# Routed attention and an ELU layer on one core: scores and value products in blocks of six, over one ring of PSUM banks

## The chip, the core and the metric

The kernel runs on one core of one Trainium2 chip. A core has a matrix engine (TensorE; its products are listed as PE and its weight loads as PEld), VectorE (DVE), ScalarE (ACT), GpSimd (POOL) and SyncE (SP, which issues DMAs here). Each engine works through its own queue in order, and engines wait for one another by semaphores. TensorE writes only to PSUM, which has eight banks of 128 partitions by 512 fp32 values in this kernel; GpSimd is given no PSUM operand anywhere in it. The metric is the device time of one execution in microseconds (us).

## The reference

Queries, keys and values have the shape batch 4, heads 8, sequence 768, head dimension 64. Every query and key is assigned to the nearest of 16 centroids of its head, and a query sees only the keys of its own cluster. The result, as 3072 tokens of 512 numbers, goes through a two-layer network with an ELU between.

```python
q_assign = argmax(einsum('bhsd,hcd->bhsc', q_n, c_n))   # q, k and centroids normalised
k_assign = argmax(einsum('bhsd,hcd->bhsc', k_n, c_n))
mask   = q_assign[:, :, :, None] == k_assign[:, :, None, :]
scores = where(mask, q @ k.T / 8, -1e9)
attn   = softmax(scores)                                  # over the keys
x      = (attn @ v) as (3072, 512)
h      = x @ w_in                                         # (3072, 2048)
g      = where(h > 0, h, exp(min(h, 0)) - 1)
out    = g @ w_out                                        # (3072, 512)
```

All arrays are fp32 in the kernel; w_in and w_out arrive as 8-byte numbers and are converted on the chip.

## The kernel before, in words

Everything that matters here is in `main_path`. The heads are taken in pairs (NPR = 4 pairs a batch, 16 in all). A pair's 768 queries are taken in two halves of HS = 384 columns, its keys in NT = 6 tiles of 128. One **score unit** is one key tile of one half of one pair, for both heads: `score` (L305) issues, for the two heads e = 0 and 1, an fp32 product of 64 rows (L311) and a bf16 product that adds the mask (L320: the key's cluster against the query's, a large negative number where they differ), each a head in its own half of the array's rows. Both heads' results lie in two neighbouring PSUM banks, and one exponential on ACT (L328) turns them into a tile `p` of 128 x 768 in SBUF. An fp32 product is issued as two instructions, so a unit has four of L311 and two of L320. `add` (L330) sums the six `p` of a half, on POOL for batch 1 and on DVE later. `values` (L340) multiplies the unit's `p` with the values, the two heads in the two halves of the array's columns (four instructions of L345), into one bank `o` over the six tiles; after the sixth ACT copies it to `xT` (L354). `divide` (L356) sums over the keys with a product with ones (L360), ACT moves the sums and keeps a check sum (L365), DVE takes the reciprocal (L366), POOL multiplies `xT` by it (L368) and keeps another sum (L369).

`mlp` (L372) is the two-layer network for one half of one batch: 16 steps `hidden` (L377; eight instructions of L383 into one bank, then exponential on ACT L392, clamp on POOL L393, and on DVE L398, which is issued one step later and still reads the bank), then three output tiles `outer` (L403), each in four parts of eight instructions (L413), a copy on ACT (L422) and a DMA out.

`prepare` (L280) plans what the next batch needs: turns of q and k by TensorE against an identity (L231, 3 transposes each) with copies on ACT (L234) and DVE (L236), similarities with the centroids (L247, L254), and the assignment on DVE (L261 to L272); `masks` (L274) makes the queries' mask operand of a pair (L278).

The order is written out by hand: `tc.manual_schedule()` keeps the order in which the program issues. The loop at L462 goes over batches b = 0 to 4, and each has 48 slots. A slot issues one score unit of batch b, then what was set for this slot with `at`: the add of one slot ago, the values of two slots ago (LAG = 2), the divide of a half that ended three slots ago; then, in the first two rounds, two steps of the weights' conversion (`weigh`, DVE and POOL, L185 to L198), then the planned steps for batch b + 1, then 1 or 2 of the 56 steps (`hidden` or `outer` part) of batch b - 1. So TensorE alternates between three tilings of its array in every slot: 64 rows x 128 columns (scores), 128 x 64 (values, divide), 128 x 128 (network, turns). The last round, b = 4, has no scores: it only finishes the network of the last batch.

PSUM is four pools: `ps_s` with 2 tiles of 2 banks for scores, `ps_b` with 2 tiles of 1 bank for `bank()` (turns, similarities, divide, hidden), `ps_o` with 1 for values and `ps_f` with 1 for the outputs; in the last round `hidden` and `outer` also take from `ps_s` and `ps_o` in turn. `p` has 6 buffers, `xT` 10, `gT` 16.

Of the kernel before, what the change touches and what calls it, by code (L numbers as in the profile page):

```python
# [9 lines left out]
F32 = mybir.dt.float32  # L10
# [50 lines left out]
def main_path(ctx, tc, c, q, k, v, centroids, moe_w_in, moe_w_out, out):  # L61
    nc = tc.nc
    B, H, S, D = q.shape
    NC = centroids.shape[1]
    DM, DF = moe_w_in.shape
    NT = S // P
    HT = NT // 2
    HS = S // 2
    NPR = H // 2
    KC = DM // P  # L70
    FC = DF // P
    SCALE = 1.0 / 8.0
# [18 lines left out]


    pairs = [(b, pr) for b in range(B) for pr in range(NPR)]
# [129 lines left out]
    T, sim, hot, qm = {}, {}, {}, {}  # L223
# [76 lines left out]
        return plan  # L300


    pu, osum, den, o_ps, xT = {}, {}, {}, {}, {}

    def score(i, half, kt):  # L305
        b, pr = pairs[i]
        s = ps_s.tile([P, 2, 512], F32, name="scores", tag="s")
        cols = slice(half * HS, (half + 1) * HS)
        for e in range(2):
            rows = slice(64 * e, 64 * e + 64)  # L310
            nc.tensor.matmul(  # L311
                s[:, e, :HS],
                lhsT=T[i, 1][rows, ts(kt, P)],
                rhs=T[i, 0][rows, cols],
                start=True,
                stop=False,
            )
        for e in range(2):
            rows = slice(64 * e, 64 * e + 64)
            nc.tensor.matmul(  # L320
                s[:, e, :HS],
                lhsT=hot[b, 1][rows, ts(kt, P)],
                rhs=qm[i][rows, cols],
                start=False,
                stop=True,
            )
        p = pu[i, half, kt] = probs.tile([P, 2, HS], F32, name="p", tag="p")
        nc.scalar.activation(p, s[:, :, :HS], Act.Exp, scale=SCALE)  # L328

    def add(i, half, kt, eng):  # L330
        if kt == 0:
            return
        if kt == 1:
            osum[i, half] = work.tile([P, 2, HS], F32, name="psum", tag="psum")
        to = osum[i, half]
        eng.tensor_tensor(  # L336
            to, pu[i, half, 0] if kt == 1 else to, pu[i, half, kt], op=Alu.add
        )

    def values(i, half, kt):  # L340
        if kt == 0:
            o_ps[i, half] = ps_o.tile([P, 512], F32, name="o", tag="o")
        o = o_ps[i, half]
        for e in range(2):
            nc.tensor.matmul(  # L345
                o[64 * e : 64 * e + 64, :HS],
                lhsT=raw["v", i][:, e, kt],
                rhs=pu[i, half, kt][:, e],
                start=(kt == 0),
                stop=(kt == NT - 1),  # L350
            )
        if kt == NT - 1:
            x = xT[i, half] = xtp.tile([P, HS], F32, name="xT", tag="xT")
            nc.scalar.copy(x, o[:, :HS])  # L354

    def divide(i, half):  # L356
        s = osum.pop((i, half))
        d = bank()
        for e in range(2):
            nc.tensor.matmul(  # L360
                d[64 * e : 64 * e + 64, :HS], lhsT=ones, rhs=s[:, e], start=True, stop=True
            )
        r = work.tile([P, HS], F32, name="r", tag="r", bufs=1)
        n = 2 * i + half
        nc.scalar.activation(r, d[:, :HS], Act.Copy, accum_out=d_sum[:, n : n + 1])  # L365
        nc.vector.reciprocal(r, r)  # L366
        x = xT[i, half]
        nc.gpsimd.tensor_tensor(x, x, r, op=Alu.mult)  # L368
        nc.gpsimd.tensor_tensor(r_sum, r_sum, r, op=Alu.add)  # L369


    def mlp(b, half, last):  # L372

        g = {}
        lag = []

        def hidden(f):  # L377
            if last and f % 2:
                h = ps_s.tile([P, 2, 512], F32, name="h2", tag="s")[:, 0, :HS]
            else:  # L380
                h = bank()[:, :HS]
            for ch in range(KC):
                nc.tensor.matmul(  # L383
                    h,
                    lhsT=w_in[:, ch, ts(f, P)],
                    rhs=xT[b * NPR + ch, half],
                    start=(ch == 0),
                    stop=(ch == KC - 1),
                )
# [12 lines left out]

        def outer(t, part, o):  # L403
            for step in lag:
                step()
            lag.clear()
            if part == 0:
                if last and t % 2:
                    o[t] = ps_o.tile([P, DM], F32, name="o2", tag="o")
                else:  # L410
                    o[t] = ps_f.tile([P, DM], F32, name="f", tag="f")
            for f in range(4 * part, 4 * part + 4):
                nc.tensor.matmul(  # L413
                    o[t],
                    lhsT=g[f][:, ts(t, P)],
                    rhs=w_out[:, f],
                    start=(f == 0),
                    stop=(f == FC - 1),
                )
            if part == 3:  # L420
                o_sb = work.tile([P, DM], F32, name="o_sb", tag="o_sb")
                nc.scalar.copy(o_sb, o[t])  # L422
# [5 lines left out]
        o = {}  # L428
# [12 lines left out]
    def weigh(n):  # L441
        for _ in range(n):
            step = next(rest, None)
            if step:
                step()
# [5 lines left out]
            step()  # L451
        weigh(1)

    LAG = 2
    slots = 2 * NPR * NT
    later = {}
    now = 0

    def at(n, step):
        later.setdefault(n, []).append(step)  # L460

    for b in range(B + 1):  # L462
        steps = []
        if b > 0:
            for half in range(2):
                steps.extend(mlp(b - 1, half, b == B))
        plan = prepare(b + 1) if b + 1 < B else {}
        done = 0
        for n in range(slots):
            if b < B:  # L470
                i, half, kt = b * NPR + n // (2 * NT), (n // NT) % 2, n % NT
                if n % (2 * NT) == LAG + 2 and i + 1 < len(pairs):
                    load("v", i + 1)
                if n % (2 * NT) == 2 * NT - 4 and pairs[i][1] + 1 < NPR:
                    masks(i + 1)
                score(i, half, kt)
                eng = nc.gpsimd if b == 0 else nc.vector
                at(now + 1, lambda i=i, half=half, kt=kt, eng=eng: add(i, half, kt, eng))
                at(now + LAG, lambda i=i, half=half, kt=kt: values(i, half, kt))
                if kt == NT - 1:  # L480
                    at(now + LAG + 1, lambda i=i, half=half: divide(i, half))
            for step in later.pop(now, []):
                step()
            if b == 0:
                weigh(2)
            for step in plan.get(n, []):
                step()
            upto = (n + 1) * len(steps) // slots
            for step in steps[done:upto]:
                step()  # L490
            done = upto
            now += 1
            if b == 1:
                weigh(2)
    weigh(1000)


# [238 lines left out]
```

## Time and profile before

| what | us |
|---|---|
| median of 3 runs | 1281.11 (1281.02 to 1281.29) |
| the profiled execution, its own time | 1280.53 |
| its span, first to last instruction | 1278.8 |
| busy: PE products | 1132.8 (89%) |
| busy: DVE | 494.5 (39%) |
| busy: POOL | 296.7 (23%) |
| busy: ACT | 281.8 (22%) |

The profile is of one execution. A line of a group names the source line, engine, operation, what it writes and reads by the program's names, the shape and the count, and then its busy time and the mean of one in ns. A line of the chain of waits has a start, a length and the work that held up the end in that time; x8 says that eight instructions stand in that piece. Matmuls overlap in the trace: a product's own duration is longer than the distance to the next one, so lengths in the chain, which go from start to start, are the ones to add up. "before" in brackets behind a line of the timeline is the idle time ahead of it and what ended it. Line numbers are those of the kernel before.

### The profile page before, as it was taken

To read this page: it belongs to the slowest core of one execution; us is meant where nothing else is said; L and a number is where in the kernel's file an instruction comes from. 1 tells how busy PE (TensorE), PEld (TensorE's weight loads), DVE (VectorE), ACT (ScalarE), POOL (GpSimd) and SP (SyncE) were. 2 spreads that over 40 slices of the span, in tenths; PEclk is the share of its full clock that TensorE was granted. 3 is DMA by queue.
4 is the path that set the end of the run, shared out by engine and by line. 5 is a ranking of instruction groups with operands and counts; after the bars stand their busy time and mean duration, and the time that the engine had idled before them with its cause. 6 is when DMAs were issued, how large, how long until landed. Compare 5 with 4: busy or idle time off the path is not lost.

```text
span 1278.8 us, 10641 instructions
## 1 busy us (share of the span) xinstructions
PE 1132.8 (89%) x4291; PEld 486.1 (38%) x4291; DVE 494.5 (39%) x596; ACT 281.8 (22%) x475; POOL 296.7 (23%) x303
## 2 busy tenths in 40 slices
PE   4644444799999999999999999999999999999998
PEld 2211111244433443344434443344434443454553
DVE  5888888833321335223321335223322332220110
ACT  2221212232212221223212321222212321110110
POOL 2476666552110220012110210012111210110110
PEclk9877777899999999999999999999999999999999
DMA  9423233010101010010100000000000000000000
GB/s 225 122 83 104 73 111 91 30 37 1 37 17 46 1 37 9 9 46 1 37 17 21 1 13 9 8 21 1 13 17 21 1 1 15 11 1 17 9 1 27
DMA packets 62793, 42.75 MB, mean 33 GB/s; under 512 B 51472, under 2 KB 55568, under 8 KB 62736
## 3 DMA queue, kind: packets, MB, share of 16 engines
q1 hardware_dynamic: 62736, 41.98, 11.5%
q8 instruction: 36, 0.59, 0.2%
q14 instruction: 21, 0.17, 0.0%
HBM read 35.68 MB, written 6.29 MB: 33 GB/s over the span
## 4 chain that ended last, share of the span: by engine, by line
PE 78%; POOL 8%; DVE 7%; issue 4%; ACT 2%; SPq 1%; DMA 0%; ACTq 0%; POOLq 0%
PE f L413 25%; PE bank L383 24%; PE scores L311 10%; PE o L345 8%; POOL psum L336 4%; PE h L383 3%; PE o L413 2%; PE scores L320 2%; DVE r L366 1%; PE bank L360 1%; PE bank L247 1%; DVE ex L187 1%; PE bank L231 1%; DVE kT L236 1%; POOL w_out L198 1%
## 5 line engine op out<-in xcount | busy, mean ns | idle before, releaser
L413 PE MATMUL f<-w_out,gT 128*128 128x512 f32 x704 | 320.4, 602 | 4.1 <-ACT o_sb L422 4.1
L383 PE MATMUL bank<-xT,w_in 128*128 128x384 f32 x896 | 314.2, 496 | 8.3 <-DVE kT L236 5.2
L328 ACT ACTIVATE p<-scores 128x768 f32<-128x768 f32 x192 | 155.8, 812 | 370.5 <-PE scores L320 363.1
L383 PEld LDWEIGHTS bank<-xT,w_in 128*128 128x128 f32 x896 | 163.1, 190 | 150.9 <-DVE gT L398 23.9
L413 PEld LDWEIGHTS f<-w_out,gT 128*128 128x128 f32 x704 | 128.3, 190 | 181.5 <-issue 171.9
L393 POOL TENSOR_SCALAR gT<-gT 128x384 f32<-128x384 f32 x128 | 64.8, 506 | 528.4 <-ACT gT L392 528.4
L311 PE MATMUL scores<-qT,kT 64*128 64x384 f32 x768 | 179.6, 545 | 0.0
L345 PE MATMUL o<-p,v_raw 128*64 128x384 f32 x768 | 170.0, 522 | 0.0
L366 DVE RECIPROCAL r<-r 128x384 f32<-128x384 f32 x32 | 81.7, 2552 | 216.5 <-ACT r L365 216.5
L398 DVE SCALAR_TENSOR_TENSOR gT<-gT,bank 128x384 f32<-128x384 f32 x112 | 61.7, 551 | 260.6 <-POOL gT L393 260.6
L336 DVE TENSOR_TENSOR psum<-psum,p 128x768 f32<-128x768 f32 x96 | 105.3, 1097 | 91.8 <-ACT p L328 91.4
L392 ACT ACTIVATE gT<-bank 128x384 f32<-128x384 f32 x112 | 55.0, 491 | 301.1 <-PE bank L383 301.1
L368 POOL TENSOR_TENSOR xT<-xT,r 128x384 f32<-128x384 f32 x32 | 46.3, 1448 | 316.0 <-DVE r L366 316.0
L360 PE MATMUL bank<-psum,ones 128*64 128x384 f32 x128 | 31.8, 579 | 91.1 <-DVE kT L236 48.9
L311 PEld LDWEIGHTS scores<-qT,kT 64*128 64x128 f32 x768 | 59.1, 188 | 121.4 <-issue 119.3
L345 PEld LDWEIGHTS o<-p,v_raw 128*64 128x64 f32 x768 | 42.2, 138 | 92.5 <-issue 92.5
L320 PE MATMUL scores<-qm,hot 64*128 64x384 bf16 x384 | 64.0, 326 | 8.2 <-DVE qm L278 8.2
L336 POOL TENSOR_TENSOR psum<-psum,p 128x768 f32<-128x768 f32 x32 | 58.8, 1837 | 1.0
L187 DVE TENSOR_SCALAR ex<-words 128x512 uint32<-128x512 uint32 x32 | 50.2, 1567 | 21.9 <-POOL w_out L198 11.5
L236 DVE COPY kT<-bank 128x384 f32<-128x384 f32 x32 | 17.1, 554 | 83.8 <-PE bank L231 83.8
L360 PEld LDWEIGHTS bank<-psum,ones 128*64 128x64 f32 x128 | 7.0, 147 | 106.8 <-issue 62.5
L369 POOL TENSOR_TENSOR r_sum<-r_sum,r 128x384 f32<-128x384 f32 x32 | 47.5, 1485 | 0.0
(78 smaller groups left out, 575.0 us busy)
## 6 DMA issues: line engine op xcount, KB each, us to landing
words<-in_moe_w_in_dram SPq DMA_DIRECT2D x16, 512.0 KB, 3.9
words<-in_moe_w_out_dram SPq DMA_DIRECT2D x16, 512.0 KB, 3.5
q_raw<-in_q_dram SPq DMA_DIRECT2D x32, 192.0 KB, 3.7
k_raw<-in_k_dram SPq DMA_DIRECT2D x32, 192.0 KB, 4.0
v_raw<-in_v_dram SPq DMA_DIRECT2D x16, 384.0 KB, 4.1
out_dram<-o_sb SPq DMA_DIRECT2D x24, 256.0 KB, 2.0
cen<-in_centroids_dram SPq DMA_DIRECT2D x1, 32.0 KB, 1.8
```

Of the source, the lines that this page charges most:

```text
L187: nc.vector.tensor_scalar(ex, high, 20, 0x7FF, op0=Alu.logical_shift_right, op1=Alu.bitwise_and)
L311: nc.tensor.matmul(s[:, e, :HS], lhsT=T[i, 1][rows, ts(kt, P)], rhs=T[i, 0][rows, cols], start=True, stop=False,)
L320: nc.tensor.matmul(s[:, e, :HS], lhsT=hot[b, 1][rows, ts(kt, P)], rhs=qm[i][rows, cols], start=False, stop=True,)
L328: nc.scalar.activation(p, s[:, :, :HS], Act.Exp, scale=SCALE)
L336: eng.tensor_tensor(to, pu[i, half, 0] if kt == 1 else to, pu[i, half, kt], op=Alu.add)
L345: nc.tensor.matmul(o[64 * e : 64 * e + 64, :HS], lhsT=raw["v", i][:, e, kt], rhs=pu[i, half, kt][:, e], start=(kt == 0), stop=(kt == NT - 1),)
L366: nc.vector.reciprocal(r, r)
L383: nc.tensor.matmul(h, lhsT=w_in[:, ch, ts(f, P)], rhs=xT[b * NPR + ch, half], start=(ch == 0), stop=(ch == KC - 1),)
L392: nc.scalar.activation(t, h, Act.Exp)
L393: nc.gpsimd.tensor_scalar(t, t, 1.0, 0.0, op0=Alu.min, op1=Alu.max)
L398: lambda: nc.vector.scalar_tensor_tensor(t, t, -1.0, h, op0=Alu.add, op1=Alu.max)
L413: nc.tensor.matmul(o[t], lhsT=g[f][:, ts(t, P)], rhs=w_out[:, f], start=(f == 0), stop=(f == FC - 1),)
```

## The change

PSUM becomes one tile `ring` of six banks and the two single banks `o_bank` and `f_bank`; `bank()` hands out the ring's banks in turn, and `banks()` two neighbours, starting at an even one. `score` takes a range of key tiles. `values` calls `divide` itself, right after its last tile. `mlp` yields eight groups a batch: per half two of eight hidden steps, each with its own `finish`, then two of six output parts, in an order in which t = 1 alone uses `f_bank` and t = 0 and t = 2 share `o_bank` with the values.

In the loop, a block of G = 6 units replaces the slot for b = 1 to 4: first the values of the last block and its divide (`flush(0)`), then six score units, the masks of the next pair, the adds, and then the eight hidden steps or six output parts of one group, with the planned steps for the next batch spread between these. For b = 0, G is 1: a slot issues its score unit, the add of the same unit, the values that are two units late (and at the sixth the divide with them), two weight steps, and the planned steps. In both, values are loaded at the slot or block that holds position 3 of a pair instead of at position 4, and masks come after the scores, at position 9 instead of 8.

```diff
-    ps_s = ctx.enter_context(tc.tile_pool(name="ps_s", bufs=2, space=PSUM))
-    ps_b = ctx.enter_context(tc.tile_pool(name="ps_b", bufs=2, space=PSUM))
-    ps_o = ctx.enter_context(tc.tile_pool(name="ps_o", bufs=1, space=PSUM))
-    ps_f = ctx.enter_context(tc.tile_pool(name="ps_f", bufs=1, space=PSUM))
+    psum = ctx.enter_context(tc.tile_pool(name="psum", bufs=1, space=PSUM))
...
+    NB = 6
+    ring = psum.tile([P, NB, 512], F32, name="ring")
+    o_bank = psum.tile([P, 512], F32, name="o_bank")
+    f_bank = psum.tile([P, 512], F32, name="f_bank")
+    turn_of = [0]
+
+    def banks():
+        turn_of[0] += turn_of[0] % 2
+        n = turn_of[0] % NB
+        turn_of[0] += 2
+        return ring[:, n : n + 2]
+
     def bank():
-        return ps_b.tile([P, 512], F32, name="bank", tag="b")
+        n = turn_of[0] % NB
+        turn_of[0] += 1
+        return ring[:, n]
...
-    def score(i, half, kt):
+    def score(i, half, kts):
...
-        s = ps_s.tile([P, 2, 512], F32, name="scores", tag="s")
+        for kt in kts:
+            s = banks()
...
     def values(i, half, kt):
-        if kt == 0:
-            o_ps[i, half] = ps_o.tile([P, 512], F32, name="o", tag="o")
-        o = o_ps[i, half]
...
-            nc.scalar.copy(x, o[:, :HS])
+            nc.scalar.copy(x, o_bank[:, :HS])
+            divide(i, half)
...
         def hidden(f):
-            if last and f % 2:
-                h = ps_s.tile([P, 2, 512], F32, name="h2", tag="s")[:, 0, :HS]
-            else:
-                h = bank()[:, :HS]
+            h = bank()[:, :HS]
...
-        def outer(t, part, o):
-            for step in lag:
-                step()
-            lag.clear()
...
+        def outer(t, part):
+            o = f_bank if t == 1 else o_bank
...
-        for f in range(FC):
-            yield lambda f=f: hidden(f)
-        for t in range(HT):
-            for part in range(4):
-                yield lambda t=t, part=part: outer(t, part, o)
+        for n in range(0, FC, FC // 2):
+            yield [lambda f=f: hidden(f) for f in range(n, n + FC // 2)] + [finish]
+        for parts in (
+            [(0, 0), (0, 1), (0, 2), (0, 3), (1, 0), (1, 1)],
+            [(2, 0), (2, 1), (2, 2), (2, 3), (1, 2), (1, 3)],
+        ):
+            yield [lambda t=t, part=part: outer(t, part) for t, part in parts]
...
+    units = 2 * NPR * NT
+    pending = []
+
+    def flush(left):
+        while len(pending) > left:
+            values(*pending.pop(0))
...
+        G = NT if b else 1
+        for n in range(0, units, G):
+            if b:
+                flush(0)
             if b < B:
                 i, half, kt = b * NPR + n // (2 * NT), (n // NT) % 2, n % NT
+                kts = range(kt, kt + G)
+                within = range(n % (2 * NT), n % (2 * NT) + G)
+                if 3 in within and i + 1 < len(pairs):
                     load("v", i + 1)
+                score(i, half, kts)
+                pending.extend((i, half, x) for x in kts)
+                if 2 * NT - 3 in within and pairs[i][1] + 1 < NPR:
                     masks(i + 1)
+                for x in kts:
+                    add(i, half, x, nc.vector if b else nc.gpsimd)
+            if b == 0:
+                flush(2)
+                weigh(2)
+            beside = [step for m in range(n, n + G) for step in plan.get(m, [])]
+            main = groups[n // G] if b else []
+            done = 0
+            for m, step in enumerate(main):
                 step()
+                upto = len(beside) * (m + 1) // len(main)
+                for other in beside[done:upto]:
+                    other()
+                done = upto
+            for other in beside[done:]:
+                other()
```

More of the change, by code (lines that the diff above doesn't have):

```diff
@@ L300, in prepare @@
         return plan
-    pu, osum, den, o_ps, xT = {}, {}, {}, {}, {}
-    def score(i, half, kt):
+    pu, osum, xT = {}, {}, {}
+    def score(i, half, kts):
         b, pr = pairs[i]
-        s = ps_s.tile([P, 2, 512], F32, name="scores", tag="s")
         cols = slice(half * HS, (half + 1) * HS)
[L309 to L328, printed above, removed]
+        for kt in kts:
+            s = banks()
+            for e in range(2):
+                rows = slice(64 * e, 64 * e + 64)
+                nc.tensor.matmul(
+                    s[:, e, :HS],
+                    lhsT=T[i, 1][rows, ts(kt, P)],
+                    rhs=T[i, 0][rows, cols],
+                    start=True,
+                    stop=False,
+                )
+            for e in range(2):
+                rows = slice(64 * e, 64 * e + 64)
+                nc.tensor.matmul(
+                    s[:, e, :HS],
+                    lhsT=hot[b, 1][rows, ts(kt, P)],
+                    rhs=qm[i][rows, cols],
+                    start=False,
+                    stop=True,
+                )
+            p = pu[i, half, kt] = probs.tile([P, 2, HS], F32, name="p", tag="p")
+            nc.scalar.activation(p, s[:, :, :HS], Act.Exp, scale=SCALE)
     def add(i, half, kt, eng):
@@ L340, in values @@
     def values(i, half, kt):
-        if kt == 0:
-            o_ps[i, half] = ps_o.tile([P, 512], F32, name="o", tag="o")
-        o = o_ps[i, half]
         for e in range(2):
             nc.tensor.matmul(
-                o[64 * e : 64 * e + 64, :HS],
+                o_bank[64 * e : 64 * e + 64, :HS],
                 lhsT=raw["v", i][:, e, kt],
@@ L372, in mlp @@
     def mlp(b, half, last):
-        g = {}
-        lag = []
+        g, lag = {}, []
         def hidden(f):
-            if last and f % 2:
-                h = ps_s.tile([P, 2, 512], F32, name="h2", tag="s")[:, 0, :HS]
-            else:
-                h = bank()[:, :HS]
+            h = bank()[:, :HS]
             for ch in range(KC):
@@ L393, in hidden @@
             nc.gpsimd.tensor_scalar(t, t, 1.0, 0.0, op0=Alu.min, op1=Alu.max)
-            for step in lag:
-                step()
-            lag.clear()
+            finish()
             lag.append(
@@ L401, in hidden, with finish @@
             )
-        def outer(t, part, o):
+        def finish():
             for step in lag:
@@ L406, in outer @@
             lag.clear()
[L407 to L411, printed above, removed]
+        def outer(t, part):
+            o = f_bank if t == 1 else o_bank
             for f in range(4 * part, 4 * part + 4):
                 nc.tensor.matmul(
-                    o[t],
+                    o,
                     lhsT=g[f][:, ts(t, P)],
@@ L421, in outer @@
                 o_sb = work.tile([P, DM], F32, name="o_sb", tag="o_sb")
-                nc.scalar.copy(o_sb, o[t])
+                nc.scalar.copy(o_sb, o)
                 nc.sync.dma_start(
@@ L426, in outer @@
                 )
-        o = {}
-        for f in range(FC):
-            yield lambda f=f: hidden(f)
-        for t in range(HT):
-            for part in range(4):
-                yield lambda t=t, part=part: outer(t, part, o)
+        for n in range(0, FC, FC // 2):
[5 more added lines that the diff above has]
+            yield [lambda t=t, part=part: outer(t, part) for t, part in parts]
     load("v", 0)
@@ L452, in main_path @@
         weigh(1)
[L454 to L460, printed above, removed]
+    units = 2 * NPR * NT
[3 more added lines that the diff above has]
+            values(*pending.pop(0))
     for b in range(B + 1):
-        steps = []
+        groups = []
         if b > 0:
             for half in range(2):
-                steps.extend(mlp(b - 1, half, b == B))
+                groups.extend(mlp(b - 1, half, b == B))
@@ L467, in main_path @@
         plan = prepare(b + 1) if b + 1 < B else {}
-        done = 0
-        for n in range(slots):
+        G = NT if b else 1
+        assert b == 0 or len(groups) == units // G
+        for n in range(0, units, G):
+            if b:
+                flush(0)
             if b < B:
                 i, half, kt = b * NPR + n // (2 * NT), (n // NT) % 2, n % NT
-                if n % (2 * NT) == LAG + 2 and i + 1 < len(pairs):
+                kts = range(kt, kt + G)
+                within = range(n % (2 * NT), n % (2 * NT) + G)
+                if 3 in within and i + 1 < len(pairs):
@@ L473, in main_path @@
                     load("v", i + 1)
-                if n % (2 * NT) == 2 * NT - 4 and pairs[i][1] + 1 < NPR:
+                score(i, half, kts)
+                pending.extend((i, half, x) for x in kts)
+                if 2 * NT - 3 in within and pairs[i][1] + 1 < NPR:
                     masks(i + 1)
[L476 to L479, printed above, removed]
@@ L480, in main_path @@
-                if kt == NT - 1:
-                    at(now + LAG + 1, lambda i=i, half=half: divide(i, half))
-            for step in later.pop(now, []):
-                step()
[L484 to L492, printed above, removed]
+                for x in kts:
+                    add(i, half, x, nc.vector if b else nc.gpsimd)
@@ L493, in main_path @@
             if b == 1:
-                weigh(2)
+                weigh(2 * G)
     weigh(1000)
```

## The prediction

> **What bounds the kernel now.** I read the page first (TensorE busy 89%, every other engine below 40%), then the busy time of each engine in six stretches, cut where the first score of a batch starts on PE.
>
> ```profile
> 0.00:46.00 46.00, 19.78 (x124) 10.58 (x125) 31.91 (x72) 7.41 (x13) 10.52 (x17) 0.91 0.76 181
> 46.00:258.50 212.50, 116.47 (x603) 40.34 (x601) 177.80 (x192) 48.55 (x76) 136.03 (x105) 0.76 0.29 87
> 258.50:547.20 288.70, 280.77 (x1076) 118.81 (x1074) 92.03 (x104) 69.22 (x118) 49.16 (x53) 1.00 0.08 21
> 547.20:835.90 288.70, 280.62 (x1074) 118.72 (x1073) 92.01 (x104) 69.59 (x118) 40.77 (x48) 1.00 0.06 17
> 835.90:1104.60 268.70, 266.97 (x961) 112.04 (x960) 79.28 (x83) 66.16 (x110) 42.10 (x48) 1.00 0.03 11
> 1104.60:1278.80 174.20, 168.17 (x463) 85.55 (x462) 21.43 (x41) 20.88 (x42) 18.12 (x34) 0.99 0.03 11
> ```
>
> Columns after the length: PE, PEld, DVE, ACT, POOL busy, then granted clock. Up to 258.5 us (batch 1) DVE and POOL carry the time and PE waits. In batches 2, 3 and 4 PE is busy 97 to 99% at full clock and DVE, ACT and POOL below a third. So in 846 of 1278.8 us the time is what PE's instructions cost, and the question is whether busy means working. The chain of waits answers it. One slot of batch 2:
>
> ```profile
> 424.41 2.78 PE bank L383 x8
> 427.19 0.84 PE scores L311 x4
> 428.03 0.16 PE scores L320 x2
> 428.20 0.80 PE o L345 x4
> 428.99 5.36 PE bank L383 x16
> ```
>
> The same instructions where they follow their own kind (divide sums L360 have the values' shape, 128*64):
>
> ```profile
> 1079.90 0.80 PE bank L360 x4
> 1080.70 0.65 PE o L345 x4
> ...
> 1125.75 2.58 PE h L383 x8
> 1128.33 2.58 PE bank L383 x8
> ...
> 1148.97 13.73 PE f L413 x32
> ```
>
> Eight hidden products cost 2.58 in a run and 2.78 in a slot (5.36 for sixteen, so only the first eight pay): 0.20 more. Eight output products cost 13.73/4 = 3.43 in a run, 3.63 in a slot by the same chain: 0.20. Values 0.65 in a run, 0.80 in a slot: 0.15. The four fp32 score products are two side by side in two passes; a pass of this width takes 2.58/8 = 0.3225, so 0.645 would do and 0.84 to 0.85 is paid: 0.20. The mask products that follow in the same 64*128 tiling pay nothing (0.16 for 384 columns, half of one fp32 pass). So each slot pays 0.20 + 0.15 + 0.20 = 0.55 us for three changes of the array's tiling: 64*128, 128*64, 128*128. With 48 slots that is 26.5 us a batch.
>
> The timeline shows how: the first weight load after a change starts with its own product, after 0.55 us in which PEld loaded nothing.
>
> ```profile
> 427.12 0.30 PEld L311 LDWEIGHTS scores<-qT,kT 64*128 64x128 f32 x4 [0.55 <-issue]
> 427.12 0.92 PE L311 MATMUL scores<-qT,kT 64*128 64x384 f32 x4
> ```
>
> The Trainium skill, "TensorEngine Tiling (Array Packing)", Key Properties, says that changing the tiling mode drains TensorE; it gives no figure, and the 0.55 us a slot is this trace's.
>
> **The change, part by part.**
>
> *Blocks of six.* A block is six values, one divide, six score units, then eight hidden steps or six output parts. It pays the same three changes once: per batch 8 x 0.55 = 4.4 us instead of 26.5, a gain of 22.1 for each of batches 2, 3, 4. That holds if score follows score without a change. The trace has no mask product followed by a score. Bounds: fp32 to bf16 in this tiling costs 0 (row above); a real change costs 0.20. I take 0, since both neighbours have the form 64*128 and the weight load of 128 columns, after which the next one starts 0.11 us later in the trace, fits in the mask product's 0.16. Five such boundaries a block, 24 blocks: at most 120 x 0.20 = 24 us back.
>
> *One ring instead of pairs of banks.* Batches 2 and 3 take 288.7, batch 4 without preparation 268.7: preparation costs 20.0. Its PE work is 16 turns of three transposes (two turns in a row take 0.80 in the timeline, 143.01 to 143.81: 6.4) and four similarity steps at about 1.4 (5.6): 12. The rest is waiting for one of two banks, as here:
>
> ```profile
> 402.81 2.85 PE L383 MATMUL bank<-xT,w_in 128*128 128x384 f32 x8 [0.24 <-ACT qT L234]
> 408.58 0.55 PE L231 MATMUL bank<-ident,k_raw 128*128 128x128 f32 x3 [0.65 <-DVE kT L236]
> 409.78 2.85 PE L383 MATMUL bank<-xT,w_in 128*128 128x384 f32 x8 [0.65 <-DVE kT L236]
> ```
>
> With six banks, and turns spread between hidden steps of 2.58 us, a bank is needed again only several products later, against copies of 0.5 us. I take 13 to 15 for preparation instead of 20 (a turn between full-array products 0.33 to 0.6): 6 gained in each of batches 2 and 3, between 3 and 9. Waits of L413 for the output copy (4.1 us in all on the page, six of them, two a batch) go too, since t = 1 has its own bank and always follows t = 0 or 2: 1.4 a batch. So batch 4 goes from 268.7 to 268.7 - 22.1 - 1.4 = 245.2 (-23.5), batches 2 and 3 from 288.7 to 288.7 - 22.1 - 6 - 1.4 = 259.2 (-29.5 each).
>
> *What hides the rest.* Six exponentials (L328, 812 ns) now meet six scores in 6 x 0.805 = 4.83 us on PE: nearly equal. In the slot above the exponential starts 1.1 after its unit's first product (428.23 against 427.12 in the timeline), of which 0.1 to 0.2 is the change of tiling, so 1.0 in a run. The first ends 1.8 after the block's first score; its banks are wanted by the fourth unit at 2.4. At 0.85 a piece the fourth ends at 4.4, and the first hidden step wants its bank at 4.8. ACT's two operations before them (copy L354 and L365, 0.48 and 0.68) run beside divide and the first score. DVE in a hidden block: reciprocal 2.55, five adds near 1.1, eight L398 at 0.55, two copies: about 14 of 31 us. The reciprocal now stands ahead of the adds and these ahead of L398 on DVE, so the first hidden bank is released about 10 us after the block starts; the ring asks for it after some 21. The last L398 ends about 2 us after its group; the scores that reuse its bank come after 3.9 us of values and 0.65 of divide. The six probability buffers are all read by the values before the next scores. Nothing is late there; if ACT were, see the second rival.
>
> The Trainium skill, same page, PSUM Bottleneck, speaks against the change: tiling speeds up TensorE but not the evacuation of PSUM, and the copy may become the bottleneck. The trace's 0.812 against 0.805 is that limit reached; by the rule the sum would be the second rival's, by the rows with three units of slack it is the forecast.
>
> *Batch 1.* Its slots stay, but each POOL add and each divide is issued one slot earlier against the weight steps. In the chain a pair of halves takes 28.6 + 31.1 us (first adds at 111.66, 140.25, 171.37). I replayed POOL's and DVE's queues with the trace's durations, a DVE operation that meets a POOL one ending 0.29 after it as in the rows there. Now the reciprocal stands between a weight's first part and its end, so that weight takes 10.2 us (add 1.85, reciprocal 2.5, product and r_sum 2.2, L198 1.4 in one line); the other three 6.1, 7.5, 6.05. That is 29.9 for each half: 1.3 lost in halves without turns, 1.3 gained in those with them, where the copies of kT (1.0) hide and DVE's 1.9 us wait for L365 goes. Net 0, range -6 to +8 over four pairs.
>
> *Seams.* Entering batch 2, PE has no hidden steps to put before the last divide of batch 1, and waits for POOL's adds, 1.85 each, one after the other: +3 (0 to 5). Batch 2 has four value units fewer (-2.6), since only two are pending at its start, and the last stretch four more with their divide in a run: 3.9 + 0.65 + 0.3 of values and divide, 165.0 of products, 6.1 after the last product, 175.9 against 174.2 (+1.7). There the products already run without gaps, so nothing else is gained.
>
> *Sum*, against the profiled execution's span: 1278.8 - 2 x 29.5 - 23.5 - 2.6 + 3.0 + 1.7 = 1198.4. That execution took 1280.53, 1.7 outside its span, and lies 0.6 under the median of 1281.11. 1198.4 + 1.7 is 1200.1; I forecast **1200 us**, and a later median may lie 0.6 above.
>
> **Rivals.**
> 1. *The runs of scores still pay.* Each unit pays a change because fp32 weights follow bf16 ones. For: no row shows that order. Against: the reverse order is free. Price up to 24 us: **1224 us**, or 1212 at half.
> 2. *ACT paces the scores.* If exponentials need 1.2 apiece (their latency not overlapped), the ring makes the sixth score wait 0.2 and the first hidden step 0.6 more: about 0.8 a block, 24 blocks, 19 us: **1219 us**. Against: where ACT has work waiting in the trace, two copies of 0.48 take 0.86.
> 3. *The ring is one tile, and waits go by tile.* Then a score waits for the last exponential, a hidden product for the last L398. Per unit 1.05 us (0.36 to its start, 0.81, less 0.16), 144 units: 151; per hidden step about 2 us of L392, L393, L398, 128 steps: 256. **Slower, near 1600 us.** It outweighs the 80 us of gain once more than a fifth of those waits appear. Against: w_in is one tile too, and in the trace DVE writes one piece of it (L185 at 115.43) while POOL still works on another (L198 at 115.59).
>
> **Chances.** Forecast 0.68 (1190 to 1210), rivals 1 and 2 with parts of them 0.22 (1210 to 1226), other new waits that leave some gain 0.05, rival 3 or a like dependency 0.04, a gain eaten to within 0.2% (about what a measurement can tell from no change) 0.01. The lower end takes every open term's good side (preparation 6 less, batch 1 4 less); the upper end takes rival 1 whole with 2 us of seams. Faster 0.95, same 0.01, slower 0.04.
>
> **What would show it.** In the chain after: six L345 groups at 0.65 in a row; L311 at 0.65 within a run (0.85 there is rival 1); L383 at 2.58 inside a block; batches 2, 3, 4 near 257 (its four value units fewer taken off), 259, 245; batch 1 ending near 258. Waits of L311 or L383 on L328 are rival 2, of L383 on L398 within a run rival 3. A batch 1 much longer than 258 would break the replay.

## The result and the profile after

| | before | after |
|---|---|---|
| median, us | 1281.2 (1281.02 to 1282.29) | 1692.61 (1688.85 to 1699.72) |
| ratio | 1 | 1.3215 (1.3167 to 1.3263) |
| profiled execution, its span | 1278.8 | 1686.6 |
| mean granted clock of PE | 0.956 | 0.882 |
| PE busy | 1132.8 | 1268.8 |

The kernel became 411 us slower. The forecast was 1200 us, and slower had a chance of 0.04. The stretches of the changed kernel, cut at the first score of each batch and at the last block of values (columns as in the same view of before):

```profile
0.00:291.30 291.30, 169.83 (x737) 57.26 (x737) 200.54 (x264) 57.55 (x91) 155.97 (x125) 0.81 0.33 93
291.30:696.10 404.80, 316.82 (x1072) 137.15 (x1072) 92.52 (x104) 70.48 (x118) 32.03 (x48) 0.87 0.06 15
696.10:1102.30 406.20, 318.81 (x1074) 137.65 (x1074) 93.45 (x105) 70.49 (x118) 32.03 (x48) 0.87 0.04 12
1102.30:1470.00 367.70, 289.39 (x958) 125.90 (x960) 79.72 (x83) 65.61 (x108) 32.03 (x48) 0.90 0.02 8
1470.00:1686.60 216.60, 173.96 (x454) 82.64 (x450) 21.45 (x41) 20.27 (x41) 18.16 (x34) 1.00 0.02 8
```

Every stretch is longer. Batches 2 and 3 take 405 instead of 289, PE is busy 78% of them instead of 97%, and its clock, 1.00 before, is 0.87. DVE, ACT and POOL are no busier than before: no engine became the bound. The chain of waits of the changed kernel, where a block of six scores begins, names what did (L325 is the fp32 score, L334 the mask, L342 the exponential, L356 the values, L372 the divide's product):

```profile
845.24 4.02 PE o_bank L356 x24
849.26 0.67 PE ring L372 x4
...
850.63 0.92 PE ring L325 x4
851.55 0.18 PE ring L334 x2
...
851.81 0.82 ACT p L342
...
852.67 0.92 PE ring L325 x4
```

The six values run as forecast (24 instructions in 4.02, 0.67 a unit). Then the score, the exponential and the next score stand one behind the other in the chain: the next unit, into two other banks, starts 0.04 us after the exponential of the one before has ended. Hidden steps are no better. The timeline of the changed kernel, L391 the hidden product, L400 its exponential, L401 the clamp, L404 the last step on DVE:

```profile
913.48 2.85 PE L391 MATMUL ring<-xT,w_in 128*128 128x384 f32 x8 [0.58 <-ACT gT L400]
913.51 0.51 POOL L401 TENSOR_SCALAR gT<-gT 128x384 f32<-128x384 f32 x1 [15.80 <-ACT gT L400]
916.36 0.49 ACT L400 ACTIVATE gT<-ring 128x384 f32<-128x384 f32 x1 [2.94 <-PE ring L391]
...
916.96 0.55 DVE L404 SCALAR_TENSOR_TENSOR gT<-gT,ring 128x384 f32<-128x384 f32 x1 [8.61 <-ACT gT L400]
917.56 0.62 PEld L391 LDWEIGHTS ring<-xT,w_in 128*128 128x128 f32 x3 [1.85 <-DVE gT L404]
917.56 0.91 PE L391 MATMUL ring<-xT,w_in 128*128 128x384 f32 x2 [1.24 <-DVE gT L404]
```

L404 at 916.96 belongs to the step before the one whose exponential ended at 916.85. It reads another bank and its operand had been ready since 914.02, when L401 ended (913.51 + 0.51); still it starts when ACT has read the ring. The next hidden step, into a third bank, starts when L404 has read it. So every user of the ring, readers among them, goes after the user before it in the program's order. That is rival 3.

### The profile page after: what moved, and what is told of

Its sections match the earlier page's. It is cut to its first block, busy times and chain, and to the rows that moved or that the text cites. A ratio compares the mean times of both kernels' runs of the same rounds, so it can differ in the third digit from the quotient of the medians.

```text
span 1686.6 us, 10901 instructions
## 1 busy us (share of the span) xinstructions
PE 1268.8 (75%) x4291; PEld 540.6 (32%) x4291; DVE 487.7 (29%) x596; ACT 284.4 (17%) x475; POOL 270.2 (16%) x303
## 4 chain that ended last, share of the span: by engine, by line
PE 68%; ACT 12%; DVE 10%; issue 4%; POOL 4%; SPq 0%; DMA 0%; DVEq 0%; ACTq 0%; POOLq 0%
PE ring L391 24%; PE o_bank L417 14%; PE ring L325 11%; ACT p L342 7%; PE f_bank L417 7%; PE o_bank L356 6%; DVE gT L404 4%; ACT gT L400 3%; PE ring L334 2%; PE ring L244 2%; POOL psum L350 2%; PE ring L260 1%; PE ring L372 1%; DVE ex L200 1%; DVE ex L204 1%
## 5 line engine op out<-in xcount | busy, mean ns | idle before, releaser
L391 PE MATMUL ring<-xT,w_in 128*128 128x384 f32 x1024 | 400.9, 539 | 136.9 <-DVE gT L404 108.0
L325 PE MATMUL ring<-qT,kT 64*128 64x384 f32 x768 | 233.4, 693 | 148.4 <-ACT p L342 117.3
L391 PEld LDWEIGHTS ring<-xT,w_in 128*128 128x128 f32 x1024 | 200.7, 206 | 336.2 <-DVE gT L404 161.3
L417 PE MATMUL o_bank<-w_out,gT 128*128 128x512 f32 x512 | 238.8, 623 | 0.0
L404 DVE SCALAR_TENSOR_TENSOR gT<-gT,ring 128x384 f32<-128x384 f32 x128 | 70.5, 554 | 521.5 <-ACT gT L400 521.5
L342 ACT ACTIVATE p<-ring 128x768 f32<-128x768 f32 x192 | 155.7, 811 | 380.4 <-PE ring L334 335.5
L401 POOL TENSOR_SCALAR gT<-gT 128x384 f32<-128x384 f32 x128 | 65.0, 507 | 652.7 <-ACT gT L400 652.7
L325 PEld LDWEIGHTS ring<-qT,kT 64*128 64x128 f32 x768 | 72.6, 231 | 286.8 <-ACT p L342 228.9
L356 PE MATMUL o_bank<-p,v_raw 128*64 128x384 f32 x768 | 150.4, 526 | 0.0
L400 ACT ACTIVATE gT<-ring 128x384 f32<-128x384 f32 x128 | 62.9, 491 | 477.2 <-PE ring L391 477.2
L417 PEld LDWEIGHTS o_bank<-w_out,gT 128*128 128x128 f32 x512 | 101.1, 202 | 130.8 <-issue 130.3
L417 PE MATMUL f_bank<-w_out,gT 128*128 128x512 f32 x256 | 113.6, 594 | 0.0
L334 PE MATMUL ring<-qm,hot 64*128 64x384 bf16 x384 | 80.1, 410 | 24.0 <-DVE qm L291 24.0
L356 PEld LDWEIGHTS o_bank<-p,v_raw 128*64 128x64 f32 x768 | 50.8, 143 | 86.0 <-issue 85.9
L334 PEld LDWEIGHTS <-hot 64*128 64x128 bf16 x384 | 24.0, 116 | 64.1 <-issue 47.0
```

The source lines that it names most:

```text
L325: nc.tensor.matmul(s[:, e, :HS], lhsT=T[i, 1][rows, ts(kt, P)], rhs=T[i, 0][rows, cols], start=True, stop=False,)
L334: nc.tensor.matmul(s[:, e, :HS], lhsT=hot[b, 1][rows, ts(kt, P)], rhs=qm[i][rows, cols], start=False, stop=True,)
L356: nc.tensor.matmul(o_bank[64 * e : 64 * e + 64, :HS], lhsT=raw["v", i][:, e, kt], rhs=pu[i, half, kt][:, e], start=(kt == 0), stop=(kt == ...
L391: nc.tensor.matmul(h, lhsT=w_in[:, ch, ts(f, P)], rhs=xT[b * NPR + ch, half], start=(ch == 0), stop=(ch == KC - 1),)
L404: lambda: nc.vector.scalar_tensor_tensor(t, t, -1.0, h, op0=Alu.add, op1=Alu.max)
L417: nc.tensor.matmul(o, lhsT=g[f][:, ts(t, P)], rhs=w_out[:, f], start=(f == 0), stop=(f == FC - 1),)
```

## The experiments

**Three tiles instead of one.** Same six banks, same order of the program, same instructions. A tile is now two banks, and a user of a single bank takes a whole tile, so that turns go round three tiles instead of six banks.

```diff
-    ring = psum.tile([P, NB, 512], F32, name="ring")
+    three = [psum.tile([P, 2, 512], F32, name=f"two{n}") for n in range(3)]
...
+    def banks():
+        turn_of[0] += 1
+        return three[turn_of[0] % 3]
+
+    def bank():
+        return banks()[:, 0]
```

> The changed kernel with the same six banks as three tiles of two banks, one tile for each score unit, hidden step, turn, similarity or divide (a single-bank user leaves its tile's other bank unused). The order of the program is the changed kernel's. Theory T, the semaphores' waits go by tile and the ring is one tile, so each user of the ring waits for the last reader of any bank: the waits of L325 on L342 and of L391 on L404 go, the three long batches take about 257, 259 and 245 us, total about 1200 us (1190 to 1226, the forecast's range). Rival A, ACT or another engine paces the runs of six whatever the banks: stays above 1300. Rival B, the clock that falls while PE is in blocks is the cause by itself: stays above 1400.

Measured: **1199.36 us** (1198.61 to 1201.36), 0.9364 of before (0.9348 to 0.9379). Its stretches, from the first score of batch 2 on, the last one starting with the last values:

```profile
267.20:523.50 256.30, 256.30 (x1074) 128.05 (x1072) 99.65 (x104) 69.78 (x118) 41.61 (x48) 1.00 0.09 24
523.50:779.30 255.80, 255.80 (x1074) 127.62 (x1072) 99.86 (x104) 69.45 (x118) 41.60 (x48) 1.00 0.07 19
779.30:1018.50 239.20, 239.20 (x934) 119.40 (x932) 87.00 (x83) 64.95 (x108) 41.57 (x48) 1.00 0.03 11
1018.50:1195.00 176.50, 170.39 (x480) 87.04 (x478) 21.57 (x41) 20.88 (x42) 18.14 (x34) 1.00 0.03 11
```

PE is busy for the whole of batches 2 to 4, and the list of waits shows none on PE from 270 us to the end. The clock is back at 1.00. Theory T holds; A and B fall, since the blocks and their order are unchanged. The chain inside a block (L319 score, L328 mask):

```profile
648.33 0.84 PE two L319 x4
649.18 0.16 PE two L328 x2
649.34 0.65 PE two L319 x4
649.98 0.16 PE two L328 x2
...
653.38 6.65 PE two L385 x20
```

The first score pays the change of tiling (0.84), those behind it do not (0.65 and 0.16): the forecast's 0.805 a unit, and its first rival is gone.

**Banks packed into the three tiles.** Now two single-bank users share a tile, in different banks. The banks are handed out in the same turn as in the changed kernel, so that against that one only the tile that a bank belongs to differs. The edit against the run with three tiles:

```diff
     def banks():
-        turn_of[0] += 1
-        return three[turn_of[0] % 3]
+        turn_of[0] += turn_of[0] % 2
+        n = turn_of[0] % 6
+        turn_of[0] += 2
+        return three[n // 2]
...
     def bank():
-        return banks()[:, 0]
+        n = turn_of[0] % 6
+        turn_of[0] += 1
+        return three[n // 2][:, n % 2]
```

> Three tiles of two banks as in the first run of this group, but single-bank users take the banks in turn, so that two hidden steps in a row share a tile while standing in different banks. If waits go by tile: every second hidden step waits for the exponential of the one before it, about 0.6 us (0.49 and the way to it), 64 of 128 steps, 40 us, and some 10 us at turns, so 1240 to 1260. If waits go by bank within a tile: the same time as the first run, 1200.

Measured: 1271.36 us, 0.9921 (0.9901 to 0.994); 72 us more than with a tile for each and 421 less than the changed kernel. The timeline of this kernel, L389 the hidden product, L398 its exponential:

```profile
411.44 2.85 PE L389 MATMUL two<-xT,w_in 128*128 128x384 f32 x8
414.33 0.49 ACT L398 ACTIVATE gT<-two 128x384 f32<-128x384 f32 x1 [1.97 <-PE two L389]
...
414.87 2.85 PE L389 MATMUL two<-xT,w_in 128*128 128x384 f32 x8 [0.58 <-ACT gT L398]
```

The second step of a tile waits until ACT has read the first one's bank. In the trace a hidden step follows directly on another at 102 places. At 54 of them both stand in one tile, and the second is at least 0.74 us further behind the first than with a tile for each; at the other 48 the second stands in another tile and is no further behind. So the waits go by tile, not by bank. The price was 72 us where about 50 was expected. By the distances from one product's start to the next, 49 of it lie between hidden products (0.74 at 52 places and two longer waits, where 64 of 0.6 had been expected, and 6 us at half speed within steps), 16 at turns, 3 in batch 1.

**The ring with the old order.** The kernel before, slots and all; only scores and single banks come from one tile of six.

```diff
-        s = ps_s.tile([P, 2, 512], F32, name="scores", tag="s")
+        s = banks()
...
-        return ps_b.tile([P, 512], F32, name="bank", tag="b")
+        n = turn_of[0] % NB
+        turn_of[0] += 1
+        return ring[:, n]
```

In eight of the 128 hidden steps the ring comes round to the same bank before the step's last operation has read it, so that operation reads the next step's sums. The numbers that come out are then wrong; the instructions and their order are those of the kernel before.

> The kernel before with its order of slots, of which only the PSUM changes: the pools for scores and single banks become the one tile of six banks, handed out as in the change. Theory T: in the slots with a hidden step, the score waits for that step's L392 and the L398 before it (1.26 us in the changed kernel's trace), and the hidden step for the slot's exponential (1.05 less the 0.8 of values between), about 1.5 us in 82 slots, 125 us; turns 15; 32 hidden steps of the last stretch 40. About 1460 us. Rival: the loss comes from the blocks of six, not from the ring: 1281, or some us less.

Measured: 1546.6 us, 1.2068 (1.2044 to 1.2092). The ring alone costs 265 us with no block in sight. The size was expected too low. In its timeline both the second of two hidden steps (L392) and the next score (L323) wait for L407, the last operation of a hidden step:

```profile
335.29 2.85 PE L392 MATMUL ring<-xT,w_in 128*128 128x384 f32 x8 [1.24 <-DVE gT L407]
339.38 0.92 PE L323 MATMUL ring<-qT,kT 64*128 64x384 f32 x4 [1.24 <-DVE gT L407]
```

From hidden step to score the starts are 106 us further apart in all, between hidden products 63, before divides 24, and batch 1 is 34 longer; the last two had not been counted.

**The blocks with the old pools.** Order of the change, PSUM of before: two tiles of two banks for scores, two single ones.

```diff
+    ps_s = ctx.enter_context(tc.tile_pool(name="ps_s", bufs=2, space=PSUM))
+    ps_b = ctx.enter_context(tc.tile_pool(name="ps_b", bufs=2, space=PSUM))
...
     def banks():
-        turn_of[0] += turn_of[0] % 2
-        n = turn_of[0] % NB
-        turn_of[0] += 2
-        return ring[:, n : n + 2]
+        return ps_s.tile([P, 2, 512], F32, name="two", tag="s")
...
     def bank():
...
+        return ps_b.tile([P, 512], F32, name="bank", tag="b")
```

> The changed order (blocks of six) with the PSUM pools of before: two tiles of two banks for scores, two single banks, and the two banks for values and outputs. Theory T with a depth of two: a score waits for the exponential of two units ago, so units come 1.02 us apart instead of 0.805 (0.805 + 0.36 + 0.81 + 0.06 for two), 0.9 us a block, 24 blocks: 1221. If depth does not matter: 1200. If the blocks are slow by themselves: above 1281.

Measured: 1231.34 us, 0.961 (0.9594 to 0.9626). The order alone is worth 4%; six banks shared as three pairs, instead of two pairs for scores and two single banks, are worth another 32 us. A run of six scores takes 5.83 us here (570.98 to 576.81 in its chain) and 5.05 with three tiles (648.33 to 653.38), 0.78 a block or 19 us where 0.9 was expected; another 9.5 us, which had not been counted, lie between turns and the hidden products behind them, which wait again for one of two single banks.

**One tile for the scores alone.** As in the last run, but the four score banks are one tile.

```diff
+    four = psum.tile([P, 4, 512], F32, name="four")
...
-        return ps_s.tile([P, 2, 512], F32, name="two", tag="s")
+        n = turn_of[0] % 4
+        turn_of[0] += 2
+        return four[:, n : n + 2]
```

> Blocks of six with the old two single banks, 1231 us in that run, but the four score banks are one tile instead of two of two. Then only the scores' part of the loss is left: 1.13 us at each of 120 boundaries, 132 us against the 11 there now, and the slow score passes, 50 to 55: about 1231 + 121 + 52 = 1404. The rest up to 1692, some 290, would be the hidden steps, turns and the entry of a block. If the two parts are not additive (the clock falls for the hidden steps' waits), less than 1370.

Measured: 1410.44 us, 1.0998 (1.0976 to 1.102), six over what was expected. The scores' share of the loss is 179 us over the run above, of which 123 stand at the 120 boundaries between units, where 121 was expected. The passes of scores and masks at half speed take 27, about half of the 50 to 55 that were expected; output and hidden products at half speed, which had not been counted, take another 27. So the sum came out partly by luck. The clock in batches 2 and 3 is 0.91 and 0.94.

**Waits filled with work.** The changed kernel with its ring, and five extra products after a score unit, while the next one waits.

```diff
+            if len(kts) > 1 and kt < NT - 1:
+                for _ in range(5):
+                    nc.tensor.matmul(
+                        o_bank[:, :HS],
+                        lhsT=hot[b, 1][:64, ts(kt, P)],
+                        rhs=qm[i][:64, cols],
+                        start=True,
+                        stop=True,
+                    )
```

> The changed kernel with its one ring, and after each score unit but a block's last five extra bf16 products of 64 rows into the bank of the values, which is free at that time; the results are overwritten by the next start of an accumulation. 0.8 us at full clock, less than the wait of 1.13 us that stands there. If PE's falling clock in the broken runs costs time of its own (score passes of 0.79 instead of 0.42 us in the changed kernel's trace, 55 us in all, and 13 in the output products), the kernel gets faster with more work: 1620 to 1650. If the clock is not helped, the extra products take 1.6 us each time, 0.5 more than the wait, 120 times: about 1750. If only the waits count: 1692.

Measured: 1588.3 us, 104 us less than the changed kernel, with 600 products more. Its batches 2 and 3:

```profile
288.20:658.00 369.80, 314.07 (x1272) 144.12 (x1272) 93.26 (x104) 70.48 (x118) 32.04 (x48) 0.99 0.06 17
658.00:1029.10 371.10, 315.98 (x1272) 144.83 (x1272) 93.42 (x104) 70.49 (x118) 32.05 (x48) 0.98 0.05 13
```

The clock is 0.99 and 0.98 where it was 0.87, and 35 us a batch are gone. At full clock a score unit still takes 2.04 us from start to start (896.68 to 898.72 in its chain, 850.63 to 852.67 in the changed kernel's); what is gone are the passes at half speed. So the fall of the clock is an effect of the waits with a price of its own, and a higher one than expected. Of the 100 us between the two spans, 52 stand at scores and masks and 13 at output products, near what was expected, and 25 within hidden steps, which had not been counted (eight products from 907.41 on stand with 5.49 us in the changed kernel's timeline, the next eight with 2.85).

**Batch 1 and the seam.** With three tiles batch 2 starts at 267.2 us, before at 258.5. Two runs ask where that lies. First, adds and divides of batch 1 one slot later, as before:

```diff
-                    add(i, half, x, nc.vector if b else nc.gpsimd)
...
             if b == 0:
+                while held:
+                    divide(*held.pop())
                 flush(2)
+                while late:
+                    add(*late.pop(), nc.gpsimd)
+                late.append((i, half, kt))
```

> Three tiles as in the first run, and in batch 1 the adds and divides are issued one slot later against the weight steps, as in the kernel before. If the new order of POOL and DVE in batch 1 costs what batch 1 is longer by (267.2 against 258.5 at the first score of batch 2): about 1191 to 1194. If the two orders come out even, as the forecast's replay has it, and the difference lies where batch 2 begins: 1199, 2 either way.

Measured: 1200.07 us (1199.2 to 1200.88), the same; the first score of batch 2 stands at 268.6. The two orders come out even: with the old one the last score of batch 1 stands 1.6 us earlier (256.64 against 258.24), and PE then waits 7.3 instead of 4.3 us for POOL's adds. Second, the divide at the start of batch 2 behind the first six scores:

```diff
-            divide(i, half)
+            if (i, half) == (NPR - 1, 1):
+                held.append((i, half))
+            else:
+                divide(i, half)
...
                 score(i, half, kts)
+                while held:
+                    divide(*held.pop())
```

> Three tiles as in the first run, 1199.4 us there, and the one divide that stands at the start of batch 2's first block is issued after the block's six scores instead of before them. In the trace of the first run PE waits there from 261.5 to 265.7 for POOL's adds. If that wait is the seam's price, it hides behind 5 us of scores: 4 us less, and 0.4 more for the change of tiling: about 1195.5. If something else ends last there (the exponentials, the masks), 1199.

Measured: 1199.22 us (1198.29 to 1200.23): nothing gained. Batch 2 starts at 261.7, 5.5 us earlier, and gives it back in the same block. The timeline of this kernel, L390 the hidden product, L238 a turn, L403 the last operation of a hidden step:

```profile
272.76 0.49 PE L238 MATMUL two<-ident,q_raw 128*128 128x128 f32 x3
277.86 7.12 PE L390 MATMUL two<-xT,w_in 128*128 128x384 f32 x16 [4.61 <-DVE gT L403]
```

The reciprocal starts at 268.3 here and at 268.0 with three tiles, since POOL's adds end no earlier; DVE's five adds stand behind it in the queue, and L403, which frees a tile, behind these. The wait went from the divide to the third hidden step. So the 4 us that were expected did not come, and what ended last in their place was none of the operations named then (the exponentials, the masks) but DVE's queue.

## Why the prediction was wrong, point by point

**The step that failed** is the weighing of rival 3: "The ring is one tile, and waits go by tile." Its mechanism was described and its price worked out (near 1600 us). Yet the sum let a bank be free as soon as its own last reader was done, put the waits of the ring at nothing, and gave rival 3 a chance of 0.04, all on one piece of evidence: in the trace of before, DVE writes one piece of w_in while POOL works on another. w_in lies in SBUF. The ring lies in PSUM, and the three-tile and packed runs show that there a wait goes by the tile. No row of before has a PSUM tile with two users in different banks, so the trace could not decide; the forecast took a row from another memory for one of this. Whether it is the memory that makes the difference, no run tests. What stood in place of nothing was 491.5 us of span, the changed kernel against three tiles. By the forecast's own figures, 407 us of loss from a third mechanism that no PSUM row excluded was the largest open term, and it should have carried a large part of the chance and the upper end.

**The price of rival 3** was partly right by luck. By the table below, the waits come to about 367 us where 407 was worked out: 161 at scores (151 in the forecast) and 182 at hidden steps, turns and the entry of their runs (256 in the forecast, which took 2 us a step where the median is 1.40), with 24 in batch 1 that the forecast did not have. It did not have the half clock either, 115 us in the table. The run with filled waits took 1588 us, near the 1600, but it still has 22 us of half speed within hidden steps.

Where the loss lies, by the distance between the starts of neighbouring PE products, changed kernel against three tiles (same instructions in the same order):

| between | us more |
|---|---|
| mask and next score, 120 | 143 |
| divide and first score | 18 |
| hidden products, from step to step | 135 |
| hidden products at half speed within a step | 47 |
| turns and entry of hidden runs | 47 |
| score passes, masks and output products at half speed | 68 |
| batch 1 | 24 |

These are 482 of the 491.5 us between the two spans. The mask-to-score distance grew by 1.13 us, from 0.156 to a median of 1.284; 1.05 was worked out (the terms in its bracket add up to 1.01), for 144 units where 120 follow another.

**The rest of the forecast** is what the three-tile kernel measured:

- *Three changes of tiling a slot, 0.55 us, paid once a block.* Right: scores in a run 0.65 + 0.16, values 0.67 a unit, hidden products 2.58.
- *Batches 2, 3, 4 near 257, 259, 245.* 256.3, 255.8 and, up to the last block's products, 239.2. Batch 2 is right by luck. It has the same 1074 products as batch 3, since the pending values stand before its first score; so the four value units (2.6 us) that the forecast takes off it are not missing, and without them its size was 3 us too high, like that of batch 3. Batch 4, cut there, lacks six value units and a divide (4.02 + 0.65 in a block's chain), which stand in the last stretch; with them it takes 243.9, 1.3 less than forecast. Preparation then costs 255.8 - 243.9 = 11.9 us, where 13 to 15 was taken: the 12 us of work on PE and no waiting.
- *The Trainium skill's rule on the evacuation of PSUM* ("TensorEngine Tiling (Array Packing)", PSUM Bottleneck) did not bind with three tiles, where PE waits for no exponential. With two pairs of banks it did, by 0.78 a block.
- *Batch 1 even.* Right for the queues: reciprocals stand 29.7 and 29.9 us apart in the three-tile kernel (104.83, 134.57, 164.51), 29.9 in the replay, and putting the old order back changed nothing.
- *The seam, +3.* Mis-sized: batch 2 starts 8.7 later. The last score of batch 1 stands 1.5 later already (258.24 against 256.74), the two pending value units that now come first take 1.3, the wait for POOL's add 4.3, and the divide behind it, at half speed, 1.5. The gains above make up for it: 1199.4 against 1200.

## What to carry to other kernels

Before banks or buffers are joined into one tile, ask by what unit the framework's waits go, and take the answer from a row of the same memory; where there is none, it is an open term at its full price, and one small kernel settles it. Give each independent user of PSUM a tile of its own and take turns between tiles, not inside one. Gathering products of one tiling pays what the chain shows between a run and a mixture: here, of 1281 us, 50 with two results in flight and 82 with three pairs of banks shared by all users.

## What the runs showed of the hardware

PE's clock fell where the gaps stood between score units. In batches 2 and 3 of the changed kernel PE was busy 78% of the time and the granted clock was 0.87; in its last stretch, where hidden steps wait for one another, PE was busy 80% and the clock was 1.00. So the share of idle time alone does not decide. In a run of scores 0.96 us of idling follows 1.10 us of products at full clock (0.92 and 0.18 in the chain); in the last stretch 1.24 us follows 2.85:

```profile
852.67 0.92 PE L325 MATMUL ring<-qT,kT 64*128 64x384 f32 x4 [0.96 <-ACT p L342]
...
1478.82 2.85 PE L391 MATMUL ring<-xT,w_in 128*128 128x384 f32 x8 [1.24 <-DVE gT L404]
```

After such gaps the second of a unit's two passes of scores started about 0.8 us behind the first in 53 of 144 units, and 0.42 behind it in 80. With one tile for the scores alone the clock in batches 2 and 3 was 0.91 and 0.94. With the ring in the old order, gaps of 1.24 us after 2.85 or 4.83 us of work, it was 0.98 to 1.00 in the four stretches from 292.9 us on (cut at 620, 950 and 1250). Filling the gaps between score units with discarded products brought it to 0.99 and 0.98 and made the kernel 104 us faster. What measure of PE's work the clock follows, no run here settles.

The Trainium skill, "TensorE: Matmul & The Clock Gate", A second HAM failure mode: psum-queue depth-cycling, says that short idling of PE between groups of products can make the clock swing between half and full; the runs agree, with a mean of 0.87 and score passes near 0.42 and near 0.8 us. A row of the same page's table under Why this matters for your kernels asks that PE not idle for more than about 3 us between bursts. In batches 2 to 4 and the last stretch of the changed kernel no wait of PE lasted over 1.8 us, and the clock fell all the same: here that is not enough, and the measurement decides.
